# Loading q, k and v of an attention kernel as transfers of 120 and of 8 partitions

## The chip, the cores and the metric

The kernel runs on one core of a Trainium2 chip. The metric is the device time of one execution in microseconds (us), lower is better. Each kernel was run several times, and the executions of two kernels that are compared were taken in the same rounds on the same chip. A run that is over 1.5% above the fastest of its kernel is marked slow.

The engines are called as in the profile: PE is TensorE, PEld its weight load, DVE is VectorE, ACT is ScalarE, POOL is GpSimd, SP is SyncE. L104 is line 104 of the kernel that the profile is of.

## The reference, cut to what matters

Eight batches, each with eight heads of 576 rows and 64 columns. Attention runs within chunks of 64 rows; its result, as a matrix of 576 x 512 for each batch, goes through a token-mixing layer.

```python
def _attn_ref(q, k, v):                    # q, k, v: (8, 8, 576, 64) float32
    ...                                    # q_c, k_c, v_c: chunks of 64 rows
    scores = scale * np.matmul(q_c, k_c.transpose(0, 1, 2, 4, 3))
    ...                                    # softmax over the last axis
    out = np.matmul(attn, v_c)

def _moe_ref(x, w_q, w_k, w_out):          # x: (8, 576, 512)
    W_tok = scale * np.einsum('bsd,btd->bst', x @ w_q, x @ w_k)
    mixed = np.einsum('bst,btd->bsd', W_tok, x)
    return np.maximum(mixed, 0.0) @ w_out
```

So the kernel reads 28.3 MB of q, k and v (8 x 8 x 576 x 64 x 4 bytes, three times) and writes 9.4 MB.

## The kernel before

GpSimd issues all loads, since they convert float32 to float16 on the way. Each batch has five: q and k in two parts of 5 and 4 pieces along the free axis, and v in one. Batch 0 has v in two halves, which makes six. That is 41 loads of q, k and v in all, each over all 128 partitions, and 4 loads of weights.

```python
    TR = ((0, 5), (5, NT))                 # NT = 9
    ...
    def load_qk(b, part):
        a, e = TR[part]
        for src, dst in ((qf, qn), (kf, kn)):
            nc.gpsimd.dma_start(
                dst[b][part][:],           # 128 partitions x (e - a) x 256, float16
                src[b].rearrange("(t p r) d -> p t (r d)", p=P, r=R)[:, a:e, :],
            )

    def load_v(b, lo, hi):
        nc.gpsimd.dma_start(
            vt[b][:, lo:hi, 0:D],          # 128 partitions x (hi - lo) x 64, float16
            vf[b].rearrange("(t p) d -> p t d", p=P)[:, lo:hi, :],
        )

    load_qk(0, 0)
    load_v(0, 0, NV // 2)                  # NV = 36
    load_qk(0, 1)
    load_v(0, NV // 2, NV)
    ...                                    # weights: wqd twice, wk, wout
    for b in range(1, B):
        load_qk(b, 0)
        load_v(b, 0, NV)
        load_qk(b, 1)
```

Every load has its own tile, so no load waits for a buffer. What holds GpSimd back is seen in the instructions of the built program: it has eight semaphores for loads and uses them in turn, and each issue first waits until the load eight issues earlier has landed. So at most eight transfers are in flight.

What follows on the loads is a fixed order of units: DVE transposes q and k (`tr`), PE computes the scores of a batch (`scores`), ACT their exponential, PE the product with v (`attend`), and then the mixing layer, interleaved over batches so that PE has work while others wait.

The softmax here doesn't subtract the row's maximum and nothing guards it: scores larger than these inputs give would overflow.

Of the kernel before, what the change touches and what calls it, by code (L numbers as in the profile page):

```python
# [34 lines left out]
def kernel(  # L35
# [10 lines left out]
    nc = tc.nc  # L46
    B, H, S, D = q.shape
    DM = moe_w_out.shape[0]
    DH = moe_w_q.shape[1]
    P = 128  # L50
# [3 lines left out]
    R = 4  # L54
# [13 lines left out]
    def each(n, shape, dt, name):  # L68
        return [sb.tile(shape, dt, name=f"{name}{i}") for i in range(n)]
# [3 lines left out]
    vt = each(B, [P, NV, W], F16, "vt")  # L73
# [24 lines left out]
    vf = v.rearrange("b h s d -> b (h s) d")  # L98
    of = out.rearrange("b s m -> (b s) m")

    def load_qk(b, part):
        a, e = TR[part]
        for src, dst in ((qf, qn), (kf, kn)):
            nc.gpsimd.dma_start(  # L104
                dst[b][part][:],
                src[b].rearrange("(t p r) d -> p t (r d)", p=P, r=R)[:, a:e, :],
            )

    def load_v(b, lo, hi):
        nc.gpsimd.dma_start(  # L110
            vt[b][:, lo:hi, 0:D],
            vf[b].rearrange("(t p) d -> p t d", p=P)[:, lo:hi, :],
        )

    nc.vector.memset(zero[:], 0.0)
    load_qk(0, 0)
    load_v(0, 0, NV // 2)
    load_qk(0, 1)
    load_v(0, NV // 2, NV)
    make_identity(nc, ident[:])  # L120
    wqv = moe_w_q.rearrange("(i p) j -> p i j", p=P)
# [4 lines left out]
# [4 lines that stand above are left out]
# [187 lines left out]
    for u in PLAN.split():  # L317
# [4 lines left out]
        a = ring[int(slot)]  # L322
# [38 lines left out]
```

## Time and profile before

| | before |
|---|---|
| median of 4 runs | 137.39 us (136.95 to 138.39) |
| span of the profiled run | 136.6 us |
| PE busy | 108.6 us, 79% |
| GpSimd busy | 44.8 us, 33% |
| mean granted PE clock | 0.888 of full speed |
| batch of loads | lands every 10.0 us |
| PE waits called "issue" | 12.9 us in 10 waits |

The profiled run took 138.67 us and was marked slow, 1.3 us above the median.

First, lines of the profile's page. The first three are rows of 40 slices of 3.4 us each; a digit is the busy share of the slice in tenths (for PEclk the granted clock). The other two are the queues of the loads and of the instructions: packets, MB, and the summed time of the packets as a share of 16 engines' span, which can exceed 100% as several packets of one engine overlap.

```profile
PE   6621893799777859995978597689998999999980
...
PEclk9995559559999595999599999959999999999999
DMA  0999999999999999999999999629999322242774
...
q0 software_dynamic: 58064, 14.88, 110.9%
...
q8 instruction: 19, 0.31, 0.9%
```

DMA stands at 9 from the first microseconds to 88 us: the loads run without a break for two thirds of the span. PE has holes in that time and almost none afterwards.

Next, the chain of waits (the work that ended last, followed back), in order of time: start, length in us, what.

```profile
11.48 11.31 DMA kn<-in_k_dram
22.81 1.31 DVE kT L150
...
36.58 1.54 issue
...
43.62 1.25 issue
...
74.51 2.26 issue
```

Until 22.8 us the chain hangs on loads: batch 1's first k tile lands at 22.79 us and is transposed at once. From there to 36.58 us the chain is work without a pause over 0.05 us. Later its pauses are called "issue", time in which PE waits for nothing that the profile shows. What PE waits for, in all: us in total, times, longest.

```profile
PE ring L173 <- issue: 7.8, 5, 2.3
...
PE ring L204 <- issue: 3.4, 4, 1.5
...
PE ring L277 <- issue: 1.7, 1, 1.7
```

These 12.9 us look random until one counts instructions. In the trace the larger waits stand before PE's matmuls 608, 736, 864, 1119, 1247, 1375 and so on: some 128 matmuls with their 128 weight loads, 256 instructions, or a multiple of that, apart. Each ends 1.3 to 1.6 us after a packet of 16,384 bytes on the instruction queue has ended. This document reads them as fetches of instructions. The Trainium skill, "Runtime: NRT & Kernel Launch", "Instruction fetch mechanics", says that each engine's instruction memory is refilled in blocks of 16 KiB, 256 instructions, and that the cost is mostly hidden. While loads ran, the next fetch packet began 3.7 to 4.2 us after the end of a wait; after the wait that ended at 89.2 us, when the loads were over, 1.1 us.

GpSimd's loads, as groups of instructions (busy us, mean ns of one, then idle time before them and what ended it), and its timeline in one batch (start, length in us, then in brackets the idle time before):

```profile
L104 POOL DMA_DIRECT2D qn<-in_q_dram x16 | 13.0, 814 | 16.5 <-DMA vt<-in_v_dram 15.1
...
L110 POOL DMA_DIRECT2D vt<-in_v_dram x9 | 15.4, 1707 | 4.2 <-DMA kn<-in_k_dram 3.3
```

```profile
36.30 0.85 POOL L104 DMA_DIRECT2D qn<-in_q_dram  x1 [3.04 <-DMA vt<-in_v_dram]
...
39.22 1.85 POOL L110 DMA_DIRECT2D vt<-in_v_dram  x1 [0.74 <-DMA kn<-in_k_dram]
```

GpSimd waits some 3 to 5 us of each 10 for earlier loads to land. The view of the DMA issues (count, KB each, median us from issue to landing) shows how deep the queue is:

```profile
vt<-in_v_dram POOLq DMA_DIRECT2D x7, 576.0 KB, 16.6
qn<-in_q_dram POOLq DMA_DIRECT2D x8, 320.0 KB, 13.8
```

### The profile page before, as it was taken

To read this page: it belongs to the slowest core of one execution; us is meant where nothing else is said; L and a number is where in the kernel's file an instruction comes from. 1 tells how busy PE (TensorE), PEld (TensorE's weight loads), DVE (VectorE), ACT (ScalarE), POOL (GpSimd) and SP (SyncE) were. 2 spreads that over 40 slices of the span, in tenths; PEclk is the share of its full clock that TensorE was granted. 3 is DMA by queue.
4 is the path that set the end of the run, shared out by engine and by line. 5 is a ranking of instruction groups with operands and counts; after the bars stand their busy time and mean duration, and the time that the engine had idled before them with its cause. 6 is when DMAs were issued, how large, how long until landed. Compare 5 with 4: busy or idle time off the path is not lost.

```text
span 136.6 us, 5492 instructions
## 1 busy us (share of the span) xinstructions
PE 108.6 (79%) x2479; PEld 66.8 (49%) x2479; DVE 78.3 (57%) x132; ACT 67.9 (50%) x117; POOL 44.8 (33%) x51
## 2 busy tenths in 40 slices
PE   6621893799777859995978597689998999999980
PEld 2221672644464524572646254456665577563430
DVE  3245773387749706993757387826898888720000
ACT  3003301476526543373537264643785776659970
POOL 6998686266274383382572000000000000000000
PEclk9995559559999595999599999959999999999999
DMA  0999999999999999999999999629999322242774
GB/s 8 155 173 175 186 201 161 186 197 160 191 192 162 194 190 162 196 185 168 199 178 172 195 178 173 83 80 367 334 381 340 130 82 82 77 151 84 260 274 163
DMA packets 63275, 24.66 MB, mean 181 GB/s; under 512 B 39700, under 2 KB 58644, under 8 KB 63252
## 3 DMA queue, kind: packets, MB, share of 16 engines
q0 software_dynamic: 58064, 14.88, 110.9%
q1 hardware_dynamic: 5188, 9.44, 18.6%
q8 instruction: 19, 0.31, 0.9%
q14 instruction: 4, 0.03, 0.1%
HBM read 29.75 MB, written 9.44 MB: 287 GB/s over the span
## 4 chain that ended last, share of the span: by engine, by line
PE 66%; issue 11%; DMA 8%; POOL 7%; DVE 4%; ACT 1%; DVEq 0%; POOLq 0%
PE ring L297 25%; PE ring L173 10%; DMA kn<-in_k_dram 8%; PE ring L227 7%; PE ring L237 6%; PE ring L204 6%; PE ring L277 5%; PE ring L263 5%; PE ring L249 3%; POOL qn L104 2%; POOL kn L104 1%; POOL vt L110 1%; DVE xt L232 1%; DVE kT L150 1%; DVE xn L214 1%
## 5 line engine op out<-in xcount | busy, mean ns | idle before, releaser
L297 PE MATMUL ring<-wout,rmx 128*128 128x512 f16 x144 | 38.5, 405 | 0.2
L181 ACT ACTIVATE est<-ring 128x640 f16<-128x640 f32 (+1 forms) x32 | 19.8, 651 | 26.9 <-PE ring L173 26.3
L173 PE MATMUL ring<-qT,kT 32*64 32x64 f16 x1152 | 16.2, 215 | 16.2 <-issue 7.8
L214 DVE TENSOR_TENSOR xn<-ring,rec 128x640 f16<-128x640 f32 x32 | 26.4, 824 | 1.2
L285 ACT ACTIVATE rmx<-ring 128x576 f16<-128x576 f32 x32 | 19.9, 653 | 6.7 <-PE ring L277 6.6
L173 PEld LDWEIGHTS <-kT 32*64 32x64 f16 x1152 | 13.4, 114 | 20.1 <-issue 9.6
L150 DVE STREAM_TRANSPOSE kT<-kn 128x640 f32<-128x640 f32 (+1 forms) x16 | 19.3, 1207 | 4.7 <-DMA kn<-in_k_dram 4.7
L297 PEld LDWEIGHTS <-rmx 128*128 128x128 f16 x144 | 13.1, 101 | 15.5 <-issue 4.2
L104 POOL DMA_DIRECT2D qn<-in_q_dram x16 | 13.0, 814 | 16.5 <-DMA vt<-in_v_dram 15.1
L232 DVE COPY xt<-ring 128x1280 f16<-128x1280 f16 x16 | 13.0, 821 | 9.3 <-PE ring L227 9.1
L213 DVE RECIPROCAL rec<-ring 128x10 f32<-128x10 f32 x32 | 6.7, 209 | 18.7 <-PE ring L204 17.6
L110 POOL DMA_DIRECT2D vt<-in_v_dram x9 | 15.4, 1707 | 4.2 <-DMA kn<-in_k_dram 3.3
L204 PE MATMUL ring<-vt,est 64*64 64x65 f16 x576 | 12.4, 210 | 4.4 <-issue 3.4
L150 DVE STREAM_TRANSPOSE qT<-qn 128x640 f32<-128x640 f32 (+1 forms) x16 | 12.3, 767 | 6.0 <-DMA qn<-in_q_dram 6.0
L104 POOL DMA_DIRECT2D kn<-in_k_dram x16 | 12.9, 805 | 7.6 <-DMA kn<-in_k_dram 3.9
L204 PEld LDWEIGHTS <-est 64*64 64x64 f16 x576 | 8.7, 118 | 10.8 <-issue 7.4
L227 PE MATMUL ring<-ident,xn 128*128 128x128 f16 x160 | 13.3, 243 | 0.0
L309 ACT COPY kn<-ring 128x512 f32<-128x512 f32 x16 | 9.4, 589 | 7.6 <-PE ring L297 7.4
L309 ACT COPY qn<-ring 128x512 f32<-128x512 f32 x16 | 9.4, 588 | 7.4 <-PE ring L297 5.9
L227 PEld LDWEIGHTS <-xn 128*128 128x128 f16 x160 | 11.2, 111 | 2.1 <-issue 1.3
L244 ACT CAST wqT<-ring 128x576 f16<-128x576 f32 x8 | 5.1, 639 | 14.0 <-PE ring L237 14.0
L237 PE MATMUL ring<-xt,wqd 128*128 128x288 f16 x64 | 10.7, 316 | 0.0
(30 smaller groups left out, 74.9 us busy)
## 6 DMA issues: line engine op xcount, KB each, us to landing
out_dram<-qn SPq DMA_DIRECT2D x16, 256.0 KB, 3.3
out_dram<-kn SPq DMA_DIRECT2D x16, 256.0 KB, 3.4
vt<-in_v_dram POOLq DMA_DIRECT2D x7, 576.0 KB, 16.6
qn<-in_q_dram POOLq DMA_DIRECT2D x8, 320.0 KB, 13.8
kn<-in_k_dram POOLq DMA_DIRECT2D x8, 320.0 KB, 14.1
qn<-in_q_dram POOLq DMA_DIRECT2D x8, 256.0 KB, 16.0
kn<-in_k_dram POOLq DMA_DIRECT2D x8, 256.0 KB, 16.0
out_dram<-spare SPq DMA_DIRECT2D x4, 256.0 KB, 2.0
```

What stands on the lines that cost most here:

```text
L104: nc.gpsimd.dma_start(dst[b][part][:], src[b].rearrange("(t p r) d -> p t (r d)", p=P, r=R)[:, a:e, :],)
L110: nc.gpsimd.dma_start(vt[b][:, lo:hi, 0:D], vf[b].rearrange("(t p) d -> p t d", p=P)[:, lo:hi, :],)
L150: nc.vector.transpose(out=o, in_=src[b][part].bitcast(F32).rearrange("p t (r d) -> p t r d", d=32))
L173: nc.tensor.matmul(a[CH * ch : CH * ch + CH, i, (t - t0) * CH : (t - t0) * CH + CH], lhsT=k_of(b, t, 2 * rows + i, ch, e), rhs=q_of(b, t, ...
L181: nc.scalar.activation(est[b % 2][s].rearrange("p i t c -> p i (t c)")[:, :, 0:n], a[:, :, 0:n], AF.Exp, scale=scale_attn,)
L204: nc.tensor.matmul(a[CH * (c % 2) : CH * (c % 2) + CH, hh, jj * W : jj * W + D + 1], lhsT=lhsT, rhs=rhs, start=True, stop=True,)
L214: nc.vector.tensor_tensor(out=xn[b % 2][:, :, 2 * kk * D : 2 * kk * D + 2 * D].rearrange("p j (i d) -> p i j d", i=2), in0=xv[:, :, :, 0:D ...
L227: nc.tensor.transpose(tx[:, i, j * P : j * P + P], xn[b % 2][:, j, (2 * n + i) * P : (2 * n + i) * P + P], ident[:],)
L237: nc.tensor.matmul(a[:, h, 0:HS], lhsT=wqd[:, i, :], rhs=xt[b % 2][i // 2][:, i % 2, h * HS : h * HS + HS], start=(i == 0), stop=(i == NI ...
L285: nc.scalar.activation(rmx[(b // 2) % 2].rearrange("p (h i) n -> p i h n", h=2)[:, i, :, o : o + HS], a[:, :, 0:HS], AF.Relu, scale=scale_moe,
L297: nc.tensor.matmul(a[:, 0, :], lhsT=rmx[pr % 2][:, i, tl * P : tl * P + P], rhs=wout[:, i, :], start=(i == 0), stop=(i == NI - 1),)
L309: nc.scalar.copy(os_, a[:, 0, :])
```

## The change

Each load of q, k and v becomes two: one of partitions 0 to 119 and one of partitions 120 to 127. The bytes, their places and everything that PE, DVE and ACT do stay as they were. 41 loads become 82.

```diff
     def load_qk(b, part):
         a, e = TR[part]
         for src, dst in ((qf, qn), (kf, kn)):
+            for x, y in ((0, 120), (120, P)):
+                nc.gpsimd.dma_start(
+                    dst[b][part][x:y],
+                    src[b].rearrange("(t p r) d -> p t (r d)", p=P, r=R)[x:y, a:e, :],
+                )
+
+    def load_v(b, lo, hi):
+        for x, y in ((0, 120), (120, P)):
             nc.gpsimd.dma_start(
-                dst[b][part][:],
-                src[b].rearrange("(t p r) d -> p t (r d)", p=P, r=R)[:, a:e, :],
+                vt[b][x:y, lo:hi, 0:D],
+                vf[b].rearrange("(t p) d -> p t d", p=P)[x:y, lo:hi, :],
             )
-
-    def load_v(b, lo, hi):
-        nc.gpsimd.dma_start(
-            vt[b][:, lo:hi, 0:D],
-            vf[b].rearrange("(t p) d -> p t d", p=P)[:, lo:hi, :],
-        )
```

## The prediction

> **What bounds the kernel now**, from the busy slices, the chain of waits and the timeline:
>
> 1. 0 to 32 us: loads. The chain has one 11.3 us link, the landing of batch 1's first k tile at 22.8 us; VectorE transposes it at once. Batch 2's first k tile (landed 32.23, used 32.25) has no slack either.
> 2. 32 to 91 us: loads keep the DMA engines busy (9 in each slice; one batch lands every 9.8 us), but have slack: batch 3's first k tile lands 42.0, is used 44.7; batch 7's last lands 88.9, is used 109.1. TensorE is held by "issue" waits of 0.9 to 2.3 us, 12 us together. Each ends 1.4 to 1.6 us after a 16 KB packet of the instruction queue; these come every 6.4 us while loads run. I read them as instruction fetches delayed by load traffic: the Trainium skill, "Runtime: NRT & Kernel Launch", "Instruction fetch mechanics", says that refill comes in 16 KiB blocks and is normally hidden. The trace agrees on the size, not on the hiding. After 91 us there are no such waits.
> 3. 91 us to the end: TensorE at work 41.2 of 45.6 us.
>
> **What the change does.** Bytes, compute and the order on PE, VectorE and ScalarE stay. 41 loads become 82.
>
> - GpSimd: an issue costs about 0.64 us plus 0.26 ns a descriptor (fitted to 0.75, 0.85, 1.24, 1.84 us in the timeline), so 41 more cost about 26 us on top of 44.8. GpSimd now waits 3 to 5 us a batch for earlier landings; five more issues need 3.2. It should fit, barely.
> - Depth: the program uses eight load semaphores in turn; each issue waits for the landing of the eighth load before it. Split, that is four loads in flight: issue to landing falls from 14-16 us to about 8. Enough to feed the engines, barely.
> - Spread: the Trainium skill, "DMA: Bandwidth & Descriptors", "How many engines (k)", says that some such copies take ceil(partitions/16) partitions an engine, others a divisor of the partition count on engines chosen round-robin. In the first case 120 partitions fill 15 engines with 8 each, and the 8 go one each to eight of those: the fullest has 9 for 8, one has none, and a batch takes 9.8 x 9/8 = 11.0 us. In the second the average stays even. The trace doesn't show which; I hold the first likelier (55%).
>
> **On the critical path.** First case: of 28 us of loading before 32 us, 23 are split loads: +2 to +3 us. Loads end near 100 instead of 89 us (still before use), so one or two more fetch waits: +2. Together about 142. Second case: +0.5 to +1 at the head: 138.5. A gain would come only if shallower queues leave gaps in which fetches get through: up to several of the 12 us back.
>
> **Predicted:** 140.3 us, range 136 to 144.5. Faster by over 2%: 0.15; within 2%: 0.42; slower by over 2%: 0.43.
>
> **What would show it.** GpSimd busy about 71 us, 8-partition issues 0.65 us each; issue to landing halved; batch 1's first k tile landing at 24.5 to 26 (first case) or 23.5 us; batches every 11.0 or 9.8 us; PE's issue waits as many or more; work after 91 us unchanged.
>
> **What would make it wrong.** Gaps in the loads that free the fetches (faster); 120-partition descriptors costing GpSimd much more than the fit; an engine left empty that happens to serve the fetches; PE's clock falling differently after a longer head idle.

## The result, and the profile after

The changed kernel took 143.93 us (median of 4 runs, 143.44 to 144.44) against 137.39. The ratio of the fast runs is 1.0465, 95% interval 1.0396 to 1.0535: slower. Ratios here and below are the mean time of one kernel's fast runs over that of the other's of the same rounds, so not quite the ratio of the medians that are quoted.

| | before | after |
|---|---|---|
| median | 137.39 us | 143.93 us |
| span of the profiled run | 136.6 us | 142.3 us |
| GpSimd busy | 44.8 us | 70.1 us |
| mean granted PE clock | 0.888 | 0.842 |
| batch 1's first k tile has landed | 22.79 us | 25.55 us |
| batch 1's v has landed | 26.26 us | 31.11 us |
| batch of loads lands every | 10.00 us | 12.19 us |
| the 560th matmul starts | 36.0 us | 40.0 us |
| the last load has landed | 88.9 us | 106.6 us |
| the last matmul starts | 132.4 us | 138.2 us |
| from the 560th to the last matmul | 96.4 us | 98.2 us |
| of it PE idle; PE at work | 13.0; 83.4 us | 12.7; 85.5 us |
| mean granted PE clock in it | 0.929 | 0.896 |
| PE waits called "issue" | 12.9 us in 10 | 11.8 us in 5 |

The landing times and the numbered matmuls are read from the trace, and so is PE's idle time, the sum of its gaps between matmuls. The page of the changed kernel, the same lines as before:

```profile
PE   6704695279948993999997399669969999999990
...
PEclk9975558555995599569999779968999999999999
DMA  0999999999999999999999999999933999982674
...
q0 software_dynamic: 65632, 14.91, 134.5%
...
q8 instruction: 19, 0.31, 0.9%
```

Two things stand out in q0. It has 7,568 packets more, though the bytes of q, k and v are the same. And the packets took 134.5% of 142.3 us against 110.9% of 136.6: 191.4 us for each engine in place of 151.5. By size, in the trace:

| packets of the loads | count before | mean ns | count after | mean ns |
|---|---|---|---|---|
| 128 bytes (rows of v, weights) | 38,400 | 32.4 | 38,400 | 43.0 |
| 512 bytes (q and k) | 18,432 | 60.5 | 18,432 | 68.0 |
| 4 bytes | 720 | 19.4 | 8,288 | 12.6 |

The rows of v are cut as before and there are as many of them, and their mean is a third longer. Not each of them is: the median is 32 ns in both kernels. Over 48 ns took 0.9% of the 128-byte packets before and 22.5% after, and these took 80 ns on average. So a minority of packets takes more than twice as long, and the rest are as fast as before. The 4-byte packets are counted further below.

The chain of waits after the change:

```profile
20.13 10.98 DMA vt<-in_v_dram
...
40.59 2.31 issue
...
54.44 2.60 issue
...
77.21 3.34 issue
...
91.36 2.40 issue
...
105.58 1.13 issue
```

Before, the chain's link to the loads was the k tile of batch 1, over at 22.8 us. Now it is batch 1's v, over at 31.1 us. The fetch waits go on: two of them, 2.40 and 1.13 us, are after 91 us, where there was one of 0.56 us before; loads now run to 106.6 us. What PE waits for:

```profile
PE ring L175 <- issue: 8.1, 3, 3.3
...
PE ring L206 <- issue: 3.7, 2, 2.6
...
PE ring L206 <- DMA vt<-in_v_dram: 0.9, 2, 0.5
```

There are five fetch waits in place of ten, each about twice as long; the sum is 1.1 us less. The first scores of batch 1, on PE's timeline of the kernel before and of the changed one:

```profile
24.83 1.16 PE L173 MATMUL ring<-qT,kT 32*64 32x64 f16 x80 [3.03 <-DVE qT L150]
```

```profile
27.66 1.16 PE L175 MATMUL ring<-qT,kT 32*64 32x64 f16 x80 [4.40 <-DVE qT L152]
```

They are 2.8 us later. GpSimd's groups, its timeline in one batch and the DMA issues:

```profile
L105 POOL DMA_DIRECT2D qn<-in_q_dram x32 | 22.9, 728 | 1.9 <-DMA kn<-in_k_dram 1.0
...
L112 POOL DMA_DIRECT2D vt<-in_v_dram x18 | 21.6, 1211 | 0.9 <-DMA kn<-in_k_dram 0.5
```

```profile
42.74 1.47 POOL L105 DMA_DIRECT2D kn<-in_k_dram  x2 [3.57 <-DMA vt<-in_v_dram]
44.27 2.54 POOL L112 DMA_DIRECT2D vt<-in_v_dram  x2
```

```profile
vt<-in_v_dram POOLq DMA_DIRECT2D x7, 540.0 KB, 10.6
qn<-in_q_dram POOLq DMA_DIRECT2D x8, 300.0 KB, 9.1
...
vt<-in_v_dram POOLq DMA_DIRECT2D x7, 36.0 KB, 9.0
```

GpSimd is busier by 25.3 us, but it still waits for landings (3.57 us in this batch), so it doesn't set the pace. Issue to landing fell from 14 to 17 us to 6 to 11. The DMA engines were rarely short of work: in the trace, fewer than 16 packets of the loads were in flight for 3.1% of the time from 40 to 85 us (before: 0%).

So the loss starts with the loads. From the trace, the changed kernel is 4.0 us late at the 560th matmul and 5.7 at the last one. The 1.7 us in between are not waits: PE is idle for 0.3 us less there, and at work for 2.1 us longer, at a lower granted clock. The rest of this document asks what in the two transfers makes the loads slow.

### The profile page after: what moved, and what is told of

The parts are those of the page before. It is cut to its first block, busy times and chain, and to the rows that moved or that the text cites. A ratio compares the mean times of both kernels' runs of the same rounds, so it can differ in the third digit from the quotient of the medians.

```text
span 142.3 us, 5594 instructions
## 1 busy us (share of the span) xinstructions
PE 111.3 (78%) x2479; PEld 68.5 (48%) x2479; DVE 78.5 (55%) x132; ACT 67.7 (48%) x117; POOL 70.1 (49%) x92
## 3 DMA queue, kind: packets, MB, share of 16 engines
q0 software_dynamic: 65632, 14.91, 134.5%
## 4 chain that ended last, share of the span: by engine, by line
PE 63%; DMA 17%; issue 11%; POOL 3%; ACT 2%; DVE 2%; DVEq 0%; POOLq 0%
PE ring L299 24%; DMA vt<-in_v_dram 13%; PE ring L175 8%; PE ring L229 6%; PE ring L239 6%; PE ring L206 6%; PE ring L279 5%; PE ring L265 4%; DMA kn<-in_k_dram 4%; PE ring L251 3%; POOL vt L112 1%; DVE xt L234 1%; POOL qn L105 1%; POOL kn L105 1%; ACT rmx L287 1%
## 5 line engine op out<-in xcount | busy, mean ns | idle before, releaser
L299 PE MATMUL ring<-wout,rmx 128*128 128x512 f16 x144 | 37.9, 402 | 0.2
L105 POOL DMA_DIRECT2D kn<-in_k_dram x32 | 22.6, 716 | 25.0 <-DMA vt<-in_v_dram 23.9
L175 PE MATMUL ring<-qT,kT 32*64 32x64 f16 x1152 | 16.8, 217 | 19.3 <-issue 8.1
L175 PEld LDWEIGHTS <-kT 32*64 32x64 f16 x1152 | 14.0, 117 | 23.1 <-issue 9.4
L105 POOL DMA_DIRECT2D qn<-in_q_dram x32 | 22.9, 728 | 1.9 <-DMA kn<-in_k_dram 1.0
L112 POOL DMA_DIRECT2D vt<-in_v_dram x18 | 21.6, 1211 | 0.9 <-DMA kn<-in_k_dram 0.5
L206 PE MATMUL ring<-vt,est 64*64 64x65 f16 x576 | 12.6, 213 | 5.7 <-issue 3.7
L234 DVE COPY xt<-ring 128x1280 f16<-128x1280 f16 x16 | 12.9, 817 | 6.1 <-PE ring L229 5.7
L229 PE MATMUL ring<-ident,xn 128*128 128x128 f16 x160 | 13.4, 242 | 0.3 <-DVE xn L216 0.3
L239 PE MATMUL ring<-xt,wqd 128*128 128x288 f16 x64 | 11.2, 329 | 0.0
```

What stands on the lines that cost most here:

```text
L105: nc.gpsimd.dma_start(dst[b][part][x:y], src[b].rearrange("(t p r) d -> p t (r d)", p=P, r=R)[x:y, a:e, :],)
L112: nc.gpsimd.dma_start(vt[b][x:y, lo:hi, 0:D], vf[b].rearrange("(t p) d -> p t d", p=P)[x:y, lo:hi, :],)
L175: nc.tensor.matmul(a[CH * ch : CH * ch + CH, i, (t - t0) * CH : (t - t0) * CH + CH], lhsT=k_of(b, t, 2 * rows + i, ch, e), rhs=q_of(b, t, ...
L206: nc.tensor.matmul(a[CH * (c % 2) : CH * (c % 2) + CH, hh, jj * W : jj * W + D + 1], lhsT=lhsT, rhs=rhs, start=True, stop=True,)
L229: nc.tensor.transpose(tx[:, i, j * P : j * P + P], xn[b % 2][:, j, (2 * n + i) * P : (2 * n + i) * P + P], ident[:],)
L239: nc.tensor.matmul(a[:, h, 0:HS], lhsT=wqd[:, i, :], rhs=xt[b % 2][i // 2][:, i % 2, h * HS : h * HS + HS], start=(i == 0), stop=(i == NI ...
```

## The experiments

All of them are edits of the kernel before, except e_112, e_64, e_head, e_late, e_turn16 and e_turn9, which are edits of the changed one. All gave a correct result. 17 kernels ran, in five sessions; the kernel before was timed in each, with medians of 137.54, 137.24, 137.34, 137.34 and 137.80 us. One execution of the kernel before in the fourth session took 460.81 us and is not counted. Here is what came of them; the batch is the time from one batch's last load to the next one's, and the packet is that of 128 bytes (the mean), both from the trace. By the record's rule, which asks for 2%, the change, e_vonly, e_v104, e_turn16 and e_turn9 are slower, e_best1 and e_best2 faster, e_pool and e_64 the same; the others are unclear, or, in e_v112, without a verdict. An interval that leaves out 1 does show a difference, and that of e_head lies above 1.02. The profiles of e_112, e_plus8_wide, e_head, e_vonly, e_v112 and e_v104 fell in runs marked slow. The sessions ran on different chips, so times of two sessions are less sure to compare than those of one.

| kernel | session | median us | ratio, 95% interval | batch, us | packet, ns |
|---|---|---|---|---|---|
| the change (120 + 8) | first result | 143.93 | 1.0465 [1.0396, 1.0535] | 12.19 | 43.0 |
| e_cols (two, each of 128) | 1 | 134.62 | 0.9757 [0.9682, 0.9832] | 10.29 | 32.5 |
| e_112 (112 + 16) | 1 | 135.67 | 0.9829 [0.9746, 0.9913] | 11.31 | 34.3 |
| e_tiny (128 and a 64-byte load) | 1 | 135.32 | 0.9725 [0.9619, 0.9831] | 10.61 | 32.6 |
| e_pool (128 and a memset) | 1 | 136.91 | 0.9938 [0.9879, 0.9997] | 10.05 | 32.3 |
| e_plus8_end | 2 | 138.07 | 1.0095 [1.0039, 1.0151] | 11.35 | 33.0 |
| e_plus8_wide | 2 | 137.31 | 0.9950 [0.9862, 1.0039] | 10.92 | 32.6 |
| e_head (change in batches 0 to 2) | 2 | 142.80 | 1.0410 [1.0313, 1.0507] | - | 35.8 |
| e_late (change in batches 3 to 7) | 2 | 136.92 | 0.9981 [0.9892, 1.0071] | - | 37.6 |
| e_64 (64 + 64) | 3 | 138.37 | 0.9961 [0.9880, 1.0042] | 10.42 | 35.7 |
| e_vonly (120 + 8, v alone) | 3 | 146.15 | 1.0524 [1.0429, 1.0619] | 11.75 | 49.3 |
| e_best1 | 3 | 133.77 | 0.9741 [0.9688, 0.9794] | - | 32.6 |
| e_best2 | 3 | 132.09 | 0.9510 [0.9435, 0.9585] | - | 32.8 |
| e_v64 (64 + 64, v alone) | 4 | 140.85 | 1.0236 [1.0133, 1.0339] | 10.35 | 36.5 |
| e_v112 (112 + 16, v alone) | 4 | 140.85 | none: one fast run | 10.55 | 36.7 |
| e_v104 (104 + 24, v alone) | 4 | 145.59 | 1.0572 [1.0466, 1.0679] | 11.67 | 54.9 |
| e_turn16 | 5 | 154.81 | 1.1290 [1.1201, 1.1378] | 14.59 | 41.1 |
| e_turn9 | 5 | 157.55 | 1.1399 [1.1280, 1.1518] | 14.97 | 42.8 |

The theory after the result: 120 and 8 partitions do not divide evenly among the 16 DMA engines, and this makes loads slow. The rivals: the number of transfers, the time of GpSimd, the shallower queue, and that a small group of partitions is cut off at all. Shares of the engines that the expectations below name, "9 for 8" among them, are those of the prediction's first case; session 4 comes back to them.

### Session 1: number of transfers, GpSimd's time, or the cut?

e_cols makes the same 82 transfers as the change, but cuts along the free axis, so that each has all 128 partitions.

```diff
-                dst[b][part][:],
-                src[b].rearrange(...)[:, a:e, :],
+            for x, y in ((a, e - 1), (e - 1, e)):
+                    dst[b][part][:, x - a : y - a],
+                    src[b].rearrange(...)[:, x:y, :],
...
+        for x, y in ((lo, hi - 2), (hi - 2, hi)):   # and so for v
```

> Every load split in two as in the change, so 82 load transfers, four loads in flight and some 25 us more issuing on GpSimd; but both parts keep all 128 partitions (the free axis is cut: 34+2 columns of v, 4+1 and 3+1 row groups of q and k), so every DMA engine has an equal share and no transfer is of 8 partitions. Theory N (the number of transfers: issue time and only four loads in flight) expects 143 to 144 us and a batch every 12.0 us, as the change. Theory S (how 120+8 partitions spread over engines and SBUF) expects 138 to 139 us and a batch every 9.9 to 10.3 us.

It took 134.62 us, faster than the kernel before. The queue of the loads in its page:

```profile
q0 software_dynamic: 58720, 14.88, 115.7%
```

Busy time of PE, PEld, DVE, ACT and POOL with the number of instructions, then the clock, the DMA share and GB/s, from 36 to 91 us: the view by windows of the kernel before, of the changed one and of e_cols.

```profile
36.00:91.00 55.00, 42.64 (x1127) 27.53 (x1130) 34.71 (x54) 26.21 (x45) 20.19 (x20) 0.89 1.70 169
```

```profile
36.00:91.00 55.00, 46.01 (x1137) 29.34 (x1131) 36.25 (x56) 27.21 (x47) 35.69 (x45) 0.84 2.06 149
```

```profile
36.00:91.00 55.00, 44.53 (x1211) 29.26 (x1210) 37.50 (x61) 28.14 (x48) 36.99 (x48) 0.94 1.76 174
```

e_cols keeps GpSimd as busy as the change does (36.99 against 35.69 us), and still gets 1,211 matmuls done where the kernel before does 1,127. Twice as many transfers cost nothing; with them the kernel is 2.9 us faster (134.62 against 137.54). Not all of that is the queue: in the lines above the granted clock is 0.94 in e_cols and 0.89 before. Between e_cols and the change lie 9.3 us (143.93 - 134.62, of two sessions). The number of transfers is the same, so they come from how a load is cut, the clock included.

e_112 cuts by partitions too, but into 112 and 16, both multiples of 16.

```diff
+            for x, y in ((0, 112), (112, P)):       # and so for v
```

> Loads split into 112 and 16 partitions: both are multiples of 16, so each engine gets 7 and 1 partitions, an even share of 8, and no filler packets of 4 bytes; but the second transfer has all 16 engines write into 16 neighbouring partitions. If within theory S the uneven share (9, 8 or 0 partitions) is the cost: as e_cols, 138 to 139 us. If the crowding of one small transfer's writes into neighbouring partitions is the cost: 141 to 143 us, with 128-byte packets at the end of each v load of 60 ns or more instead of 32. Theory N: 143 to 144 us.

It took 135.67 us. Its 128-byte packets took 34.3 ns, not 43.0. So it is not the cut by partitions as such that makes packets slow, nor the small second part. Yet its batches came only every 11.31 us, and the 560th matmul started at 39.1 us, 3.1 later than before and almost as late as with the change (that profile fell in a run marked slow). Its chain hangs on the same load as the change's, batch 1's v, over at 30.5 us:

```profile
18.89 11.62 DMA vt<-in_v_dram
```

It lost at the head as the change does, with few slow packets, and won it back later: from the 560th matmul on PE was idle for 10.0 us, against 13.0 before and 12.7 with the change, and its fetch waits after 91 us were 0.56 and 0.44 us, not 2.40 and 1.13.

e_tiny leaves the 41 loads whole and adds a load of 64 bytes (16 partitions of 4 bytes) behind each, into a scratch tile. e_pool adds a memset of GpSimd in place of that load.

```diff
+        t = dump[seen["n"] % 10]                     # e_tiny, after each load
+        nc.gpsimd.dma_start(t[0:16, :], qf[0][0:16, 0:2])
...
+        nc.gpsimd.memset(burnt[:], 0.0)              # e_pool, after each load
```

> Whole loads of 128 partitions, each followed by a load of 64 bytes into a scratch tile: the same 82 issues and the same turns of the eight semaphores as the change, with no bytes moved otherwise than before. Theory N expects 143 us or more, a batch every 12 us, the stretch before each v load's first bytes empty. Theory S expects at most 139 us, a batch every 10 us.

> Whole loads as before, with a GpSimd memset of about 0.6 us after each: the change's extra time on GpSimd with no extra transfer and eight loads still in flight. If GpSimd's time by itself is a cost: 139 us or more. If not: 137 to 138 us; I expect this, since GpSimd waits for landings 3 to 5 us a batch.

e_pool took 136.91 us, with GpSimd busy for 62.5 us: time on GpSimd is free here, as far as these 17.7 us more go (the change adds 25.3). e_tiny took 135.32 us (two of its four runs were marked slow, the fast two have a ratio of 0.9725): as in e_cols, a queue of eight transfers that holds four real loads did better than one of eight. What PE waits for in e_tiny:

```profile
PE ring L183 <- issue: 3.4, 2, 2.0
...
PE ring L214 <- issue: 2.1, 2, 1.9
...
PE ring L307 <- issue: 0.8, 1, 0.8
```

The fetch waits fell from 12.9 us to 6.3. This fits the prediction's remark that a shallower queue might let fetches through. It is not the whole matter, as session 3 shows.

### Session 2: the places of the 8 partitions, and where in time the loss is

e_plus8_end leaves the loads whole and loads the rows of partitions 120 to 127 once more, into scratch at the same partitions. e_plus8_wide puts them at partitions 3, 7 to 31 instead. If 8 partitions side by side were slow because they lie close together, the first would be slower.

```diff
+        nc.gpsimd.dma_start(t[120:P, ...], what)     # e_plus8_end, after each load
...
+        nc.gpsimd.dma_start(t[3:32:4, ...], what)    # e_plus8_wide
```

> Whole loads of 128 partitions, and after each the rows of partitions 120 to 127 loaded once more, into a scratch tile at the same partitions 120 to 127: the change's small transfer (one partition on each of eight engines, all writing into eight neighbouring partitions) beside an even main transfer; 1/16 more bytes. Theory U (the fullest engine has 9 for 8 partitions, that alone): a batch every 10.3 x 9/8 = 11.6 us, the same as the next run, about 138 to 140 us. Theory C (the writes crowd into a few partitions): a batch every 12 us or more, 128-byte packets over 60 ns at the end of each v load, 141 us or more.

> The same, but the scratch partitions are 3, 7, 11 to 31, every fourth: same engines' shares, same bytes, same source, only the writes no longer lie side by side. Theory U: equal to the run before it. Theory C: faster than it by 2 us or more, a batch every 10.3 to 11.6 us, 128-byte packets near 32 ns.

They took 138.07 and 137.31 us, ratios 1.0095 and 0.9950. The batches came every 11.35 and 10.92 us; the latter is about what the added bytes ask for, if e_cols' 10.29 us grow by 1/16 (10.9). Packets stayed at 33.0 and 32.6 ns in both. The difference of the two is small against the spread of the second (135.78 to 138.56 us), so whether close partitions cost time is not settled by this pair. In the trace v landed 5.06 us after the load before it with the 8 rows side by side and 4.20 us with them apart, so the loads themselves were slower. But transfers of 8 partitions don't make the packets of whole loads slow. By elimination, the slow packets come with the other part, of 120.

e_head has the change in batches 0 to 2 only, e_late in batches 3 to 7 only; they are edits of the changed kernel.

```diff
-            for x, y in ((0, 120), (120, P)):
+            for x, y in ((0, 120), (120, P)) if b < 3 else ((0, P),):     # e_head
+            for x, y in ((0, 120), (120, P)) if b >= 3 else ((0, P),):    # e_late
```

> The change in batches 0 to 2 only, later loads whole. If the loads matter only while nothing else bounds the kernel, up to 32 us: the whole loss of some 4 us of the head stays, with the later instruction-fetch waits as before the change: 141 to 142 us. If the loss is made later: under 139.5 us.

> The change in batches 3 to 7 only. Head as before (S of batch 1 at 25 us in TensorE's timeline, not 27.7). If the loss is the head's: 136 to 138 us, a little under before if the shallower queue frees instruction fetches. If the loss is made later: 140 us or more.

e_head took 142.80 us, 5.6 more than the kernel before in that session (137.24); e_late took 136.92, 0.3 less. They sum to 5.2 of the 6.5 us. So the loss is made by the loads of the first three batches. In this kernel slower loads in later batches cost nothing that can be measured.

### Session 3: q and k, or v; and an even cut

e_64 cuts each load into 64 and 64 partitions: as many transfers as e_cols, half of a load each.

```diff
+            for x, y in ((0, 64), (64, P)):         # and so for v
```

> Loads split into 64 and 64 partitions: the count of transfers and an even share (4 + 4 partitions an engine) as in the run of 34+2 columns, no fillers; what differs is which partitions an engine writes and that one transfer covers half of them. If it matters where a transfer's partitions lie even with even shares: a batch every 10.8 us or more, 136 us or more. If only a very small group of partitions matters: as the split by columns, 10.3 us and 134 to 135.5 us.

It took 138.37 us (136.38 to 139.71), ratio 0.9961: the same as before. It has the number of transfers of e_cols and keeps the engines supplied (fewer than 16 packets in flight for 0.1% of the time from 40 to 85 us), but it has no gain, and its fetch waits are 12.6 us. So "four loads in flight let fetches through" isn't sufficient as an explanation of the gain of e_cols, e_tiny and e_112. What those three share and e_64 lacks is a small second transfer; this is an observation, not a tested cause. On the cut itself the Trainium skill, "DMA: Bandwidth & Descriptors", "Rules for kernel authors", says of two transfers to disjoint partition halves: don't bother. This run agrees.

e_vonly applies 120 + 8 to v alone and leaves q and k whole.

```diff
     def load_v(b, lo, hi):
+        for x, y in ((0, 120), (120, P)):           # load_qk as before
```

> The change (120 and 8 partitions) on v alone; q and k whole. The intervals between landings put the whole loss on v (3.8 us before, some 5.8 us after, q and k unchanged). If so: most of the change's loss, 140 to 143 us and a batch every 11.5 to 12 us. If the loss is in all loads alike: 138 to 140 us.

It took 146.15 us, no faster than the whole change. Its queue of loads:

```profile
q0 software_dynamic: 62816, 14.90, 141.4%
```

The 128-byte packets took 49.3 ns. The 16 completions of one load of v, which in the kernel before come within 0.4 to 2.7 us, spread over up to 10.2 us: the engines drift apart. In the changed kernel, too, the time from landing to landing grew for v (3.8 to 6.1 us, with its small part) and hardly for q and k once the first batches were through. But the total of e_vonly is not the change's loss made again. Its 560th matmul started at 37.7 us, only 1.7 late where the change is 4.0 late. The rest came afterwards: PE idle for 16.1 us in place of 13.0, and at work for 87.1 in place of 83.4 at a granted clock of 0.884 (that profile, too, fell in a slow run). So splitting v alone makes packets slow and v late, but less than half of the head's loss; no run splits q and k alone.

e_best1 and e_best2 try to use what was learned: whole loads, the 64-byte load behind each only from batch 3 on, and in e_best2 also the 512 KB load of the output weights, which stood ahead of batch 1's loads, moved behind batch 1's v.

```diff
+        if b >= 3:                                   # both, after each load
+            tiny()
...
-    nc.gpsimd.dma_start(wout[:], ...)                # e_best2 alone
     for b in range(1, B):
         load_qk(b, 0)
         load_v(b, 0, NV)
+        if b == 1:
+            nc.gpsimd.dma_start(wout[:], ...)
         load_qk(b, 1)
```

> Whole loads; the 64-byte companion loads after those of batches 3 to 7 only, so eight loads are in flight during the head and four later. Head as before (S of batch 1 at 25 us), instruction-fetch waits as in the run with companions everywhere (some 6 us instead of 13): 133.5 to 134.5 us. If the depth has nothing to do with the gain: 137 us.

> As the run before it, and the 512 KB load of the output weights moved from before batch 1's loads to after batch 1's v. It was landed at 19 us and first used at 29.6 us, so batch 1's k tile and v land some 2.3 us sooner; batch 2's k tile, which has some 2 us of slack, sets the limit: 1 to 2 us faster, 132 to 133 us. If the weights then come late: no gain.

e_best1 took 133.77 us and e_best2 132.09, ratios 0.9741 and 0.9510. Both beat both kernels. In e_best2 the first k transpose and the first scores of batch 1, on the timelines of DVE and of PE:

```profile
20.00 1.35 DVE L163 STREAM_TRANSPOSE kT<-kn 128x640 f32<-128x640 f32 x1
```

```profile
22.06 0.78 PE L186 MATMUL ring<-qT,kT 32*64 32x64 f16 x64 [0.72 <-DVE qT L163]
```

They are 2.8 us earlier than before (22.81 and 24.83 us), as the chain of the kernel before promised: up to there loads bind, and the output weights stood in the way. But the lead does not last. In e_best2's chain the next link is a load again, batch 1's second k tile, over at 29.07 us:

```profile
16.55 12.52 DMA kn<-in_k_dram
```

Its 560th matmul started at 36.3 us, 0.3 later than before. The kernel is faster because of what follows: from there PE was idle for 7.9 us (13.0 before, 8.4 in e_best1) and at work for 80.1 (83.4 and 83.5), at a granted clock of 0.961 (0.929 and 0.926). That the moved load causes this is not shown. e_best2's runs lie between 130.29 and 134.29 us, so its lead over e_best1 is less sure than that over the kernel before.

### Session 4: crowded or uneven?

120 + 8 differs from 64 + 64 in two ways: the small part is crowded into 8 partitions, and neither part is a multiple of 16. 112 + 16 is crowded and a multiple; 104 + 24 is less crowded and not a multiple. All three for v alone, beside e_vonly:

```diff
     def load_v(b, lo, hi):
+        for x, y in ((0, 64), (64, P)):             # e_v64;  112: e_v112;  104: e_v104
```

> Only v split, into 64 and 64 partitions: share of the engines even (4 + 4), no small group. The control for the two runs after it: 136 to 138 us and a batch every 10.0 to 10.5 us under either theory.

> Only v split, into 112 and 16 partitions: share even (7 + 1), but sixteen engines write the second transfer into 16 neighbouring partitions. If the crowding into few partitions makes the loss of the 120 and 8 split of v (146 us): 141 us or more. If the uneven share makes it: as the run with 64 and 64.

> Only v split, into 104 and 24 partitions: [...]the second transfer is spread over 24 partitions. If the uneven share makes the loss: 142 us or more, engines some 4 to 8 us apart late in the loads, as with 120 and 8. If the crowding makes it: 136 to 139 us.

The two multiples took 140.85 us each, the other two 145.59 and 146.15. So for v alone no cost of crowding is seen, and parts that are not multiples of 16 cost about 5 us (145.59 - 140.85 and 146.15 - 140.85). Three of e_v112's runs were marked slow, its one fast run took 138.55 us; by fast runs alone e_v104 stands 0.0336 of the kernel before above e_v64 (1.0572 - 1.0236), 4.6 us. The packets tell the same: 36.5 and 36.7 ns against 54.9 and 49.3. Only a part of the time is lost at the head: at the 560th matmul the profiles of e_v64 and e_v104 are 2.5 us apart. The queues of e_v64 and of e_v104:

```profile
q0 software_dynamic: 58208, 14.88, 119.8%
```

```profile
q0 software_dynamic: 67424, 14.92, 152.4%
```

e_v104 has 9,216 packets more than e_v64, all of 4 bytes. Such counts tell how the engines were used, which the trace doesn't name. For each transfer there are 16 completion packets of 4 bytes, so 41 more transfers make 656 more, and that is exactly the growth of e_cols, of e_112 and of e_64 (720 to 1,376). The changed kernel has 8,288, which is 6,912 more than those. Each of the 8 batches has 36 + 18 = 54 rows per partition (36 of v, 9 of q, 9 of k), 432 in all, and 6,912 is 16 x 432: eight missing partitions of the 128 places of the main transfer (16 engines with 8 each) and eight of the 16 places of the small one (16 engines with 1 each). So it looks as if an engine without data got a 4-byte packet for each row that the others move. e_plus8_end fits: it adds transfers of 8 partitions to whole loads, and has 4,832 - 1,376 = 3,456 = 8 x 432. In e_v104 (288 rows of v), 9,216 is 32 x 288. With 104 partitions spread as 7 to an engine, as far as they go, 8 places would be empty, and 8 more with 24 spread as 2 to an engine: 16 x 288 = 4,608. Twice that fits 13 engines with 8 and three with none (24 places), and 12 engines with 2 and four with none (8 places).

That is the rule which the Trainium skill states in "DMA: Bandwidth & Descriptors", "How many engines (k)": the largest k up to 16 that divides the partition count, on k consecutive engines from a cursor that goes round. Its exception, ceil(partitions/16) to each of 16 engines, doesn't fit this count; expectations that rest on it fall with it, and so does "9 for 8" where it takes the same engine to be the fullest each time. That the empty engine moves is supported by one more reading: batch 1's main v transfer was issued by 20.1 us, and the first of its 16 completions came at 27.45 us. If one engine had been spared each time, it would have been far ahead.

The 4-byte packets themselves are not the loss: 6,912 of them at 9 ns (their median), over 16 engines, make 3.9 us of each engine's time, a tenth of the 39.9 us by which the packets' time grew (191.4 - 151.5). Most of it is in the packets with data.

How much of the change's loss do the uneven parts explain? The traces, side by side: when batch 1's v has landed, the GB/s of the window from 10 to 32 us, when the 560th matmul starts, and PE's idle time, its time at work and its granted clock from there to the last matmul.

| kernel | batch, us | v landed, us | GB/s | 560th, us | idle, us | at work, us | clock |
|---|---|---|---|---|---|---|---|
| before | 10.00 | 26.26 | 183 | 36.0 | 13.0 | 83.4 | 0.929 |
| e_cols | 10.29 | 27.33 | 175 | 36.7 | 11.1 | 80.8 | 0.963 |
| e_64 | 10.42 | 27.68 | 179 | 37.1 | 13.4 | 81.1 | 0.964 |
| e_112 | 11.31 | 30.51 | 159 | 39.1 | 10.0 | 83.2 | 0.927 |
| the change | 12.19 | 31.11 | 161 | 40.0 | 12.7 | 85.5 | 0.896 |
| e_v64 | 10.35 | 27.84 | 181 | 36.7 | 12.8 | 84.3 | 0.912 |
| e_v112 | 10.55 | 27.91 | 180 | 36.7 | 11.1 | 87.2 | 0.878 |
| e_vonly | 11.75 | 29.26 | 173 | 37.7 | 16.1 | 87.1 | 0.884 |
| e_v104 | 11.67 | 30.08 | 168 | 39.2 | 14.0 | 87.3 | 0.882 |

Where all loads are cut, most of the head's loss is there already with 112 + 16: 3.1 of the 4.0 us at the 560th matmul, 4.25 of the 4.85 us at batch 1's v. Parts that aren't multiples of 16 add the rest, and 0.9 of the 2.2 us that a batch takes longer. So at the head it is mainly the small group cut off, with even shares and near-normal packets, that goes with the loss. 64 + 64 has little of it. For v alone 112 + 16 has none beyond 64 + 64, so q and k must have a part in it; how is open. For 112 + 16 of all loads this rests on one trace, of a slow run. After the head the kernels differ by PE's waits and by its clock; how the cut would set these, no run here shows.

### Session 5: does the moving start make packets slow?

A theory for the slow packets: when 15 + 8 engines are used per load, each load starts one after the other at another engine, so engines work on unlike partitions and disturb each other. If a third transfer brought the turn back to where it began, packets would be fast again. e_turn9 adds to the change a 4-byte load on each of 9 partitions, since 15 + 8 + 9 = 32, if the turn goes as assumed; e_turn16 is its control, with 16 partitions, which should not move the turn.

```diff
+            tiny()      # after the two parts; t[0:16, :] in e_turn16, t[0:9, :] in e_turn9
```

> The change, and after each load a companion of 4 bytes to each of 16 partitions: it costs issue time and turns of the semaphores[...]. The control for the next run: if transfers on fewer than 16 engines start at a place that moves from one to the next (15 + 8 further each load), engines meet each other's partitions as in the change: 128-byte packets of 42 ns or more on average. 143 to 148 us, as GpSimd issues more.

> The same with companions of 9 partitions: 15 + 8 + 9 = 32[...]. If moving engines (each load puts an engine on other partitions than the load before) make the packets slow: 128-byte packets of 36 ns or less on average, engines apart by their fixed shares of 9, 8 and 1, and a batch no longer than in the control. If the moving has nothing to do with it: packets as slow as in the control, 42 ns or more.

They took 154.81 and 157.55 us, packets 41.1 and 42.8 ns. Packets stayed slow where the turn should have been back at its start, so the theory is not borne out: either it is wrong, or the engines are not chosen as it assumes. What speaks for the latter: the 16 completions of v's large part lie about as far apart in e_turn9 (1.9 to 3.9 us, batches 1 to 7) as in the change (2.2 to 3.8), though an engine that was spared each time could be expected to run ahead. Why the packets are slow when the large part of a load is on 15 or 13 engines stays open.

The pair shows another thing. With three transfers for each load and eight in flight, only 2.67 loads are under way, and the engines ran dry: in e_turn16 fewer than 16 packets were in flight for 18.8% of the time from 40 to 85 us. The kernel took about 11 us more than the change (154.81 - 143.93, of two sessions), while GpSimd, at work for 92.1 us, waited 24.3 us for loads of v to land. So the depth of eight transfers seems to matter below about four loads; GpSimd's added time was not tested apart from the depth.

## Why the prediction was right or wrong

The time was inside the range (136 to 144.5), and slower was the likeliest of the three outcomes. But the forecast move was +2.7 us (140.3 against 137.6) and the measured one +6.5, over twice as much.

**The three stages** were right. Until 32 us loads bind: e_head has almost all of the loss, and in e_best2 batch 1's start is 2.8 us earlier, until the next load binds. From 32 to 91 us PE pays for instruction fetches, and also for a granted clock below full speed. The end is at the same speed: from the 1,901st matmul to the end of the span it was 35.6 us before and 35.5 after.

**GpSimd** was right. Predicted busy 71 us, measured 70.1; e_pool and e_cols show no cost of its time.

**Depth** was right as a number, wrong as a sign. Issue to landing fell from 14-17 us to 6-11 (predicted about 8), and the engines stayed supplied. But the prediction gave more and shallower transfers no value, or a small chance of a gain. e_cols, with more and shallower transfers, is 2.9 us faster than before, if partly at a higher clock.

**Spread is the step that failed.** The prediction put it as two cases. In the first, "the fullest has 9 for 8, one has none, and a batch takes 9.8 x 9/8 = 11.0 us". In the second "the average stays even", which was worth 138.5 us. The packet counts fit the second way of choosing engines, and the batch took 12.19 us, longer than in either case. Both cases count partitions per engine and take the speed of the packets and of the transfers as fixed. The runs show two things in place of that. The mean 128-byte packet went from 32.4 ns to 43.0, and to 49 to 55 where v alone is split unevenly, because more than a fifth of them took 80 ns and more, on average, while the others kept their 32 ns. And a split with even shares and near-normal packets, 112 + 16, already takes 11.31 us for a batch and has most of the head's loss, so that the share per engine was the wrong thing to count. In the time of the kernel the term was worth 0.5 to 5 us in the prediction. Measured against kernels with as many transfers, the change is slower by 5.6 us (e_64), 8.3 (e_112) or 9.3 (e_cols), clock and fetch waits included. Which of these is its true size is open, since the controls differ among themselves.

**On the critical path.** Predicted +2 to +3 us at the head; measured +4.0 at the 560th matmul, with k at 25.55 us ("24.5 to 26", right) but v, which the prediction didn't follow, at 31.11 in place of 26.26. Predicted +2 later for "one or two more fetch waits" as loads run longer; measured +1.7, but that the numbers are close is luck. The fetch waits fell from ten to five, where "as many or more" was predicted, and their sum fell from 12.9 us to 11.8. Loads did run longer, and two waits did follow after 91 us. What made the profiled run later, however, was PE at work for 2.1 us longer, at a granted clock of 0.896 in place of 0.929.

**The clock.** The prediction named PE's clock as a risk. It was lower in the profiled run, 0.842 against 0.888. Two runs of the changed kernel with 0.842 and 0.875 took 144.08 and 143.44 us, so the clock is not what makes most of the 6.5 us. Between the two profiles it goes with the 2.1 us above; why it was lower, and how much it adds in the other runs, is open.

**What stays open**: why packets are slow when the parts aren't multiples of 16 (the trace doesn't say which engine moved a packet, so it can't show which packets met); why cutting a small group off all loads delays the head even in multiples of 16; and why a small second transfer on 16 engines gains 2 to 3 us where two halves gain nothing. Also, splitting v alone into even parts (e_v64, 1.0236) is slower than splitting all loads evenly (e_64, 0.9961). Their heads are alike and e_v64 has the lower clock (0.912 against 0.964), but no run here says why.

## What to carry to other kernels

When a load has to be split by partitions, cut it into multiples of 16: here 112 + 16 took 135.67 us and 120 + 8 took 143.93, for the same bytes and the same number of transfers. Where loads bind, don't cut off a small group either: with 112 + 16 the head was 3.1 us late, with 64 + 64 it was 1.1. Don't cost an uneven split by counting partitions per engine alone; look at what packets take before and after, at the spread as well as the mean. Before changing how loads are cut, see in the chain which load binds, and which binds next: moving one 512 KB load brought batch 1's first scores forward by 2.8 us, and by the 560th matmul the lead was gone. And compare kernels at marks along the way, not by their totals alone: the totals here mix the head's loads, the fetch waits and PE's clock.

## What the Trainium skill lacked or had wrong

- "DMA: Bandwidth & Descriptors", "How many engines (k)": the page gives an exception for some direct copies issued from GpSimd, ceil(partitions/16) partitions to an engine, and doesn't say for which. These loads, which convert float32 to float16, seem not to be among them: 104 + 24 partitions made 9,216 more 4-byte packets than 64 + 64, which fits 13 and 12 engines (the rule) and not 7 and 2 partitions to an engine (4,608).
- No page has the 4-byte packets of such transfers: 6,912 of them in the changed kernel, with a median of 9 ns, 16 for each of 432 rows.
- No page has how the packets' times change when a load is split by partitions: those of 128 bytes took 32.4 ns on average before, 43.0 with 120 + 8, 54.9 with 104 + 24 of v, and 34.3 with 112 + 16.
- "DMA: Bandwidth & Descriptors", "Rules for kernel authors", advises to coalesce many small transfers and calls those under 64 KB mostly overhead. The advice would not have helped here: 82 loads (e_cols, with second parts of 32 and 64 KB on chip) were faster than 41, by a ratio of 0.9757, and 64-byte loads added behind whole ones gave 0.9725.
- "Runtime: NRT & Kernel Launch", "Instruction fetch mechanics", calls the cost of a new 16 KiB block mostly hidden. While loads ran it was not: of the 12.9 us of PE's waits called "issue" in the kernel before, nearly all stand at multiples of 256 instructions and before 91 us.
